# Issuing a weight load ahead of the last V part, an attention score ahead of a PV, and another order of masks, casts and zeroes on DVE and Pool

## Chip, cores, metric

One core of one Trainium2 chip. The metric is device time in microseconds (us) of one launch. Each execution also lists its mean granted TensorE clock (1.0 is full speed). All runs used here are of the state "fast" unless said otherwise; verdicts are given at 2%.

## The reference

Eight batches, eight heads, 576 positions, head size 64. Sliding-window causal attention (window 64), then an MLP on the 4608 rows of 512 with d_ff 2048:

```python
mask = (rel >= 0) & (rel < 64)
attn = softmax(where(mask, q @ k.T / 8, -1e9))
x = (attn @ v) as rows of 512           # 4608 x 512
h = x @ w_in                            # 512 -> 2048
out = (h * clip(h + 3, 0, 6) / 6) @ w_out
```

## The kernel before

The engines are TensorE (PE in the views; matmuls and transposes), VectorE (DVE), ScalarE (ACT) and GpSimd (Pool); the queue of SyncE (SP) issues transfers. A head's work is named by its step and its group g of two heads: T(g) transposes q and k, S(g) makes the scores, PV(g) multiplies them with V, *norm(g)* divides by the row sums, X(g) transposes the result. 576 positions are four parts of 128 and a rest of 64; the *V tail* is that last V part.

A planner in Python keeps a clock of each engine and decides from *estimated* durations on which engine a cast or copy goes, and in which order instructions are issued. The parts that matter:

```python
QK_ENG = ((('DVE', 'ACT'), ('ACT',), ('ACT',), ('ACT',)), (("DVE", "ACT"),) * 4)   # copies of the q/k transposes
SEQ = "ppppvvvppvpvpvvvvv" "wwwwwww" "PPPPww" "PPPPVVVVV"    # order of loads: p,v batch 0; w weights; P,V batch 1
ORDER = (... ('S1', 3), ('PV', 2), ('S0', 3), ('X', 0), ('PV', 3), ...)            # attention of batch 0
...
def tqk(b, g):                    # T(g): transposes of q and k, then one copy into QKT
    ...                           # 36 transposes, L582
    copy_op("spread", QK_ENG[b][g], 2 * S, pl.t + 0.1, QK_tiles[...], tr[...], ("tr", b, g))
...
def scores(b, g, which):          # S(g): waits for ("tr", b, g); exp on ACT; masks on DVE (L634, L638)
    pl.op("DVE", t, 1.3, fn, ("mask", b, g), deps=("mask",))
...
def scores64(b, gg):              # batches 2 to 7
    pl.op("DVE", t, 0.8, ..., ("mask", b, 2 * gg + a), deps=("mask64",))           # L683
    pl.op("ACT", pl.t + 0.1, 0.82, ex, ("exp", b, gg, part), msk if part else None)
...
def pv(b, g):                     # PV(g): waits for the mask and the V casts, then norm on DVE (L737, L740)
    pl.op("DVE", pl.t + 0.1, 1.05, norm, ("op", b, g), ..., deps=(("x", m // NG, m % NG),) if m >= 0 else ())
...
for T in range(NTB):              # nine MLP blocks of 512 rows
    s1(T)                         # first stage: 64 matmuls with W_in (L811), then relu and g
    s2(T, side)                   # second stage: 64 matmuls with W_out (L859), batch T+1's attention between them
```

The softmax here doesn't subtract the row's maximum and nothing guards it: scores larger than these inputs give would overflow.

## Time and profile before

| | before |
|---|---|
| median, three runs | 307.87 us (307.68 to 308.37) |
| profiled span, its mean clock | 307.3 us, 0.994 |
| TensorE busy | 96% |
| first MLP block starts (first L811) | 22.52 us |
| block 1 starts | 60.68 us |

Read it by the starts of the blocks: the *head* ends with the first L811, *block 0* with the second, and the *steady part* is the rest.

The stage table of before, one microsecond a row (length, then busy share and number of instructions of PE, PEld, DVE, ACT and Pool; the third number from the end is the granted clock, the last two are DMA share and GB/s), shows what it is:

```profile
8.00:9.00 1.00, 0.79 (x30) 0.79 (x32) 0.67 (x3) 0.00 (x0) 0.00 (x0) 0.56 1.06 347
9.00:10.00 1.00, 1.00 (x16) 0.37 (x11) 0.38 (x2) 0.58 (x1) 0.00 (x0) 0.50 1.13 333
```

The granted clock is 1.00 until 8 us and again from 12 us; with 0.56 and 0.73 in the rows at either end, TensorE had half its clock from about 8.1 to 11.5 us, for 3.4 us, in this one execution (of 309.16 us).

### The profile page before, as it was taken

The page shows a single profiled execution, that of the slowest core. Times are in us where ns is not written, and L with a number is a line of the kernel's source. Part 1 is how long each engine was busy: PE and PEld are TensorE (multiplying, and loading weights), DVE is VectorE, ACT ScalarE, POOL GpSimd, SP SyncE. Part 2 cuts the span into 40 slices and gives each one's busy share as a digit, 9 for nine tenths or more (in the row PEclk, how much of TensorE's full clock was granted, in tenths as well). Part 3 has the DMA queues.
Part 4 walks back from the last instruction along what each step waited for, and adds up shares of the span by engine and source line. Part 5 has one row for each costly group of instructions (what it writes and reads, how often), then busy time and mean ns, then how long its engine had stood idle before and what let it go on. Part 6 is the DMA issues. An engine that isn't in the chain of part 4 may idle for free.

```text
span 307.3 us, 6640 instructions
## 1 busy us (share of the span) xinstructions
PE 294.4 (96%) x2752; PEld 154.0 (50%) x2787; DVE 162.6 (53%) x209; ACT 155.1 (50%) x190; POOL 117.6 (38%) x185
## 2 busy tenths in 40 slices
PE   6989989999999999999999999999999999999995
PEld 2554445644544454875444544454665544444443
DVE  4585676757634663466437653766275617304600
ACT  5765488365606661566156714671367236316611
POOL 3166748628914660458127622674270000000000
PEclk9799999999999999999999999999999999999999
DMA  7999999999999989999699989999990730010011
GB/s 214 254 341 391 388 338 226 250 202 289 213 196 253 282 160 159 226 281 192 149 205 284 208 129 213 266 215 140 210 218 12 120 94 0 34 70 34 0 68 71
DMA packets 134863, 58.38 MB, mean 190 GB/s; under 512 B 117296, under 2 KB 124720, under 8 KB 134832
## 3 DMA queue, kind: packets, MB, share of 16 engines
q1 hardware_dynamic: 106560, 50.80, 72.7%
q10 hardware_dynamic: 28272, 7.15, 11.8%
q8 instruction: 22, 0.36, 0.5%
q14 instruction: 9, 0.07, 0.1%
HBM read 36.70 MB, written 9.44 MB: 150 GB/s over the span
## 4 chain that ended last, share of the span: by engine, by line
PE 72%; DMA 11%; SPq 5%; DVE 3%; POOL 3%; ACT 3%; issue 2%; ACTq 0%; POOLq 0%
PE ps L811 36%; PE acc L859 31%; DMA st<-in_moe_w_out_dram 5%; DMA st<-in_v_dram 3%; SPq L357 2%; PE ps L699 2%; ACT pT L678 2%; PE ps L672 2%; DMA xT<-opg 2%; SPq L332 2%; DVE opg L740 2%; SPq L415 1%; DVE pT L683 1%; POOL V L280 1%; POOL wout L280 1%
## 5 line engine op out<-in xcount | busy, mean ns | idle before, releaser
L823 DVE SCALAR_TENSOR_TENSOR gT<-t,ps 128x1024 bf16<-128x1024 bf16 x72 | 87.7, 1221 | 96.6 <-ACT t L820 96.6
L859 PE MATMUL acc<-wout,gT 128*128 128x512 bf16 (+2 forms) x560 | 127.8, 373 | 3.2 <-issue 2.1
L811 PE MATMUL ps<-xT,win 128*128 128x512 bf16 (+4 forms) x701 | 126.1, 340 | 0.4 <-DMA xT<-opg 0.2
L820 ACT ACTIVATE t<-ps,half 128x1024 bf16<-128x1024 f32 x72 | 80.0, 1114 | 48.7 <-PE ps L811 46.7
L811 PEld LDWEIGHTS <-win 128*128 128x128 bf16 x704 | 65.2, 98 | 59.8 <-issue 0.3
L859 PEld LDWEIGHTS <-gT 128*128 128x128 bf16 x592 | 54.6, 98 | 60.7 <-issue 0.3
L877 ACT COPY osb<-acc 128x512 f32<-128x512 f32 (+2 forms) x37 | 21.4, 579 | 76.1 <-PE acc L859 70.3
L280 POOL CAST runs<-st 64x512 bf16<-64x512 f32 (+1 forms) x49 | 30.7, 626 | 69.9 <-DMA st<-in_v_dram 59.9
L280 POOL CAST nat<-st 128x512 bf16<-128x512 f32 x48 | 32.5, 698 | 12.4 <-DMA st<-in_k_dram 8.3
L678 ACT ACTIVATE pT<-ps 128x768 bf16<-128x768 f32 x36 | 26.9, 834 | 9.3 <-PE ps L672 9.3
L683 DVE TENSOR_TENSOR pT<-pT,mask 128x1152 bf16<-128x1152 bf16 x24 | 21.6, 919 | 15.5 <-ACT pT L678 15.5
L740 DVE TENSOR_TENSOR opg<-ps,rec 128x640 bf16<-128x640 f32 x32 | 26.4, 825 | 1.1
L280 POOL CAST V<-st 128x512 bf16<-128x512 f32 (+1 forms) x30 | 19.2, 641 | 3.2 <-DMA st<-in_v_dram 1.6
L622 ACT ACTIVATE pT<-ps 128x768 bf16<-128x768 f32 x16 | 12.6, 825 | 1.0 <-PE ps L613 0.8
L699 PEld LDWEIGHTS <-pT 128*64 128x64 bf16 x480 | 8.9, 111 | 6.4 <-DVE opg L740 2.5
L279 ACT COPY QKT<-ps 128x1152 bf16<-128x1152 bf16 x8 | 9.0, 1124 | 6.1 <-PE ps L582 6.1
L699 PE MATMUL ps<-runs,pT 128*64 128x65 bf16 x288 | 10.8, 197 | 0.9 <-DVE pT L683 0.8
L277 DVE CAST runs<-st 128x576 bf16<-128x576 f32 x14 | 7.2, 519 | 7.9 <-DMA st<-in_q_dram 5.5
L699 PE MATMUL ps<-V,pT 128*64 128x65 bf16 x192 | 10.2, 198 | 0.0
L672 PEld LDWEIGHTS <-QKT 64*128 64x128 bf16 x432 | 7.3, 95 | 5.1 <-issue 4.7
L280 POOL CAST wout<-st 128x1024 bf16<-128x1024 f32 x6 | 7.4, 1253 | 5.9 <-DMA st<-in_moe_w_out_dram 5.9
L582 PE MATMUL ps<-ident,runs 64*64 64x64 bf16 x288 | 7.1, 199 | 2.6 <-DVE runs L277 2.5
(60 smaller groups left out, 123.2 us busy)
## 6 DMA issues: line engine op xcount, KB each, us to landing
out_dram<-osb SPq DMA_DIRECT2D x35, 256.0 KB, 3.8
st<-in_q_dram SPq DMA_DIRECT2D x12, 512.0 KB, 7.2
st<-in_k_dram SPq DMA_DIRECT2D x24, 256.0 KB, 6.6
st<-in_v_dram ACTq DMA_DIRECT2D x24, 256.0 KB, 5.4
st<-in_moe_w_out_dram SPq DMA_DIRECT2D x4, 1024.0 KB, 13.8
st<-in_moe_w_in_dram SPq DMA_DIRECT2D x3, 1024.0 KB, 11.6
st<-in_q_dram SPq DMA_DIRECT2D x8, 288.0 KB, 6.9
st<-in_k_dram SPq DMA_DIRECT2D x8, 288.0 KB, 6.9
```

The source lines that it names most:

```text
L280: return lambda s: nc.gpsimd.tensor_copy(out=out_ap, in_=in_ap) and None
L622: nc.scalar.activation(out=pT[:, :, kbs[0] : kbs[0] + 2, 0:QW], in_=st[:, :, 0 : 2 * QW].rearrange("p h (k w) -> p h k w", k=2), func=EXP, ...
L672: nc.tensor.matmul(st[:, h, c * D : (c + 1) * D], lhsT=kwin(b, g, i, h), rhs=turned(qk(b, 0, g), i)[h * D : (h + 1) * D], start=True, stop ...
L678: nc.scalar.activation(out=pT[:, :, part * NB * D : (part + 1) * NB * D], in_=st[:, :, 0 : NB * D], func=EXP, scale=scale,)
L683: pl.op("DVE", t, 0.8, lambda s: nc.vector.tensor_tensor(out=P_half, in0=P_half, in1=mask64[:].unsqueeze(1).unsqueeze(1).to_broadcast([P, ...
L699: nc.tensor.matmul(o[odd * D : (odd + 1) * D, h, m * VW : (m + 1) * VW], lhsT=pT[:, h, i * D : (i + 1) * D], rhs=(V if i % 2 else W)[:, g, ...
L740: nc.vector.tensor_tensor(out=opg[:].rearrange("p k h d -> p h k d"), in0=ov[:, :, :, 0:D], in1=rec[:].unsqueeze(3).to_broadcast([P, 2, KB ...
L811: nc.tensor.matmul(hs, lhsT=win16[:, g, (2 * c + j) * P : (2 * c + j + 1) * P], rhs=xs, start=(g == 0), stop=(g == NG - 1),)
L820: nc.scalar.activation(out=t1[:], in_=hT[:], func=RELU, bias=half[:], scale=1.0 / 6.0)
L823: nc.vector.scalar_tensor_tensor(out=gT[:, 2 * c : 2 * c + 2, :], in0=cell["t"][:], scalar=1.0, in1=hT[:], op0=MIN, op1=MULT,)
L859: nc.tensor.matmul(accs[ts][:, c0:c1], lhsT=gT[:, fc, ts * P : (ts + 1) * P], rhs=wout16[:, fc, c0:c1], start=(fc == 0), stop=(fc == NFC - 1),
L877: nc.scalar.copy(out=osb[:, c0:c1], in_=acc[:, c0:c1])
```

## The change

The intent: fill a hole in the transfers at 14 to 16 us with W_in's first part; give TensorE S(3)'s matmuls while the V tail arrives; keep Pool free for W_in casts; load batch 1's q and k ahead of the last W_out part; and put the last mask of a batch ahead of a normalisation that does not need it. The diff, with the unchanged part of ORDER and lines with only new times cut:

```diff
-SEQ = "ppppvvvppvpvpvvvvv" "wwwwwww" "PPPPww" "PPPPVVVVV"
+SEQ = "ppppvvvppvpvpvvvvwvwwwwww" "PPPPwPPwPP" "VVVVV"
-ORDER = (... ('S1', 3), ('PV', 2), ('S0', 3), ('X', 0), ...)
+ORDER = (... ('S1', 3), ('S0', 3), ('PV', 2), ('X', 0), ...)
-    at("POOL", 17.0, 0.3, lambda: nc.gpsimd.memset(mask32[:], 1.0))     # all of Pool's masks and zeroes: 17 -> 21
+    at("POOL", 21.0, 0.3, lambda: nc.gpsimd.memset(mask32[:], 1.0))
...
-        pl.op("POOL", 0.0, 0.3, ..., ("w1", i), deps=(("T", NR6 - 1, NG - 1),))
+        pl.op("POOL", 0.0, 0.3, ..., ("w1", i), deps=(("T", NR6 - 1, NG - 1), ("cast", NR6 - 1, 2, KB - 1)))
...
-                        ("DVE", "ACT", "POOL"), V[:ss, 2 * i : 2 * i + 2, kb, :, 0:D],
+                        ("DVE",) if (i, kb) == (1, KB - 1) else ("DVE", "ACT", "POOL"), V[:ss, ...],
...
-                            ("POOL",) if i else ("DVE", "ACT", "POOL"), win16[:, :, c0 : c0 + w2],
+                            ("POOL",) if i else ("POOL",), win16[:, :, c0 : c0 + w2],
...
-            pl.op("ACT", pl.t + 0.1, 0.82, ex, ("exp", b, gg, part), msk if part else None)
+            pl.op("ACT", pl.t + 0.1, 0.75, ex, ("exp", b, gg, part), msk if part else None)
...
+        first = (("mask", b, NG - 1),) if b >= NR6 and g == 1 else ()
         pl.op("DVE", pl.t + 0.1, 1.05, norm, ("op", b, g), None if b < NXP else xdma,
-              deps=(("x", m // NG, m % NG),) if m >= 0 else ())
+              deps=first + ((("x", m // NG, m % NG),) if m >= 0 else ()))
```

One line is added, so lines from L757 on are one higher in the changed kernel (L811 is L812, L859 is L860).

More of the change, by code (lines that the diff above doesn't have):

```diff
@@ L30 @@
 QK_ENG = ((('DVE', 'ACT'), ('ACT',), ('ACT',), ('ACT',)), (("DVE", "ACT"),) * 4)
-SEQ = "ppppvvvppvpvpvvvvv" "wwwwwww" "PPPPww" "PPPPVVVVV"
-ORDER = (('T', 0), ('T', 1), ('S0', 0), ('S1', 0), ('S1', 1), ('T', 2), ('S0', 1), ('PV', 0), ('S1', 2), ('T', 3), ('S0', 2), ('PV', 1), ('S1', 3), ('PV', 2), ('S0', 3), ('X', 0), ('PV', 3), ('X', 2), ('X', 1), ('X', 3))
+SEQ = "ppppvvvppvpvpvvvvwvwwwwww" "PPPPwPPwPP" "VVVVV"
+ORDER = (('T', 0), ('T', 1), ('S0', 0), ('S1', 0), ('S1', 1), ('T', 2), ('S0', 1), ('PV', 0), ('S1', 2), ('T', 3), ('S0', 2), ('PV', 1), ('S1', 3), ('S0', 3), ('PV', 2), ('X', 0), ('PV', 3), ('X', 2), ('X', 1), ('X', 3))
 X_ENG = ((('DVE',), ('DVE', 'ACT'), ('DVE',), ('DVE', 'ACT')), (("DVE", "ACT"),) * 4)
@@ L239 @@
         out=neg[:, 2 * QW : 2 * QW + D], in_=neg32[:, 0:D]) and None, "neg", deps=("neg32",))
-    at("POOL", 17.0, 0.3, lambda: nc.gpsimd.memset(mask32[:], 1.0))
-    at("POOL", 17.1, 0.8, lambda: band(mask32, 0.0), "mask32")
+    at("POOL", 21.0, 0.3, lambda: nc.gpsimd.memset(mask32[:], 1.0))
+    at("POOL", 21.1, 0.8, lambda: band(mask32, 0.0), "mask32")
     pl.op("DVE", 26.0, 0.2, lambda s: nc.vector.tensor_copy(out=mask[:], in_=mask32[:]) and None, "mask", deps=("mask32",))
-    at("POOL", 17.2, 0.2, lambda: nc.gpsimd.memset(m64[:], 1.0))
-    at("POOL", 17.3, 0.3, lambda: nc.gpsimd.affine_select(
+    at("POOL", 21.2, 0.2, lambda: nc.gpsimd.memset(m64[:], 1.0))
+    at("POOL", 21.3, 0.3, lambda: nc.gpsimd.affine_select(
         out=m64[:], in_=m64[:], pattern=[[1, D]], compare_op=ISGE, fill=0.0, base=D, channel_multiplier=-1))
-    at("POOL", 17.4, 0.3, lambda: nc.gpsimd.affine_select(
+    at("POOL", 21.4, 0.3, lambda: nc.gpsimd.affine_select(
         out=m64[:], in_=m64[:], pattern=[[-1, D]], compare_op=ISGE, fill=0.0, base=-1, channel_multiplier=1), "m64")
@@ L250 @@
     for i, t in enumerate(W_ring):
-        pl.op("POOL", 0.0, 0.3, lambda s, t=t: nc.gpsimd.memset(t[:, :, :, :, D:VW], 1.0) and None, ("w1", i), deps=(("T", NR6 - 1, NG - 1),))
+        pl.op("POOL", 0.0, 0.3, lambda s, t=t: nc.gpsimd.memset(t[:, :, :, :, D:VW], 1.0) and None, ("w1", i), deps=(("T", NR6 - 1, NG - 1), ("cast", NR6 - 1, 2, KB - 1)))
         pl.op("POOL", 0.0, 0.6, lambda s, t=t: nc.gpsimd.memset(t[0:D, :, 0, :, :], 0.0) and None, ("w0", i), deps=(("w1", i),))
@@ L256 @@
     for t in natural:
-        at("POOL", 17.0, 0.6, zero("POOL", t[S % P : P, :, KB - 1, :]))
+        at("POOL", 21.0, 0.6, zero("POOL", t[S % P : P, :, KB - 1, :]))
     dma = {"t": 2.2, "lag": 0.2, "v": 0.0}
@@ L420, in go @@
                     casts(("cast", b, 2, i, kb), land, [(
-                        ("DVE", "ACT", "POOL"), V[:ss, 2 * i : 2 * i + 2, kb, :, 0:D],
+                        ("DVE",) if (i, kb) == (1, KB - 1) else ("DVE", "ACT", "POOL"), V[:ss, 2 * i : 2 * i + 2, kb, :, 0:D],
                         st.rearrange("p (g h d) -> p g h d", g=2, h=2), 4 * D)])
```

## The prediction

> **What bounds the kernel now.** I read the page first, then the stage table, then the timelines of the stretches where the chain of waits leaves TensorE.
>
> ```profile
> PE 294.4 (96%) x2752; PEld 154.0 (50%) x2787; DVE 162.6 (53%) x209; ACT 155.1 (50%) x190; POOL 117.6 (38%) x185
> ...
> PE 72%; DMA 11%; SPq 5%; DVE 3%; POOL 3%; ACT 3%; issue 2%; ACTq 0%; POOLq 0%
> ```
>
> TensorE is busy for 294.4 of 307.3 us, so all idle time of it together is 12.9 us. The view of waits for TensorE says to whom it goes:
>
> ```profile
> PE ps L582 <- DVE runs L277: 2.5, 4, 1.2
> PE acc L859 <- issue: 2.1, 13, 0.2
> PE ps L895 <- DVE idle L204: 1.3, 1, 1.3
> PE ps L699 <- DVE pT L683: 0.8, 3, 0.3
> PE ps L764 <- DVE opg L740: 0.6, 1, 0.6
> PE ps L712 <- ACT pT L622: 0.5, 1, 0.5
> ```
>
> The 2% line is 6.2 us away. Of the rows above, the change touches L699 (0.8), L764 (0.6), L712 (0.5) and a part of L582; the 1.3 us at the start (L895) and the 2.1 of issue stay. So the room is about 3 to 4 us if everything went right.
>
> There are three stretches. **Head**, 0 to 22.5 us: attention of batch 0, ending when the first matmul of the first MLP block (L811) starts. **Block 0**, 22.5 to 60.7 us: the MLP of block 0, with batch 1's attention threaded into its second half; the chain of waits runs through DMA there (wout landing at 35.27, V of batch 1 landing at 51.73). **Steady part**, from 60.7 us: L811 takes 13.8 us a block, 64 matmuls of 0.216 us, and nothing of it can shrink.
>
> In the head the timeline of TensorE shows its last two waits:
>
> ```profile
> 20.33 0.23 PE L712 MATMUL ps<-V,pT 128*128 128x65 bf16 x2 [0.52 <-ACT pT L622]
> ...
> 22.23 0.45 PE L764 MATMUL ps<-ident,opg 128*128 128x128 bf16 x5 [0.62 <-DVE opg L740]
> ```
>
> PV(3) waits for its exp, and the last transpose X(3) waits for the normalisation of PV(3). The stage table, one microsecond a row (last two columns: DMA share, GB/s), shows a hole in the transfers just ahead of that:
>
> ```profile
> 13.00:14.00 1.00, 1.00 (x27) 0.48 (x20) 0.02 (x1) 1.00 (x3) 0.19 (x1) 1.00 0.97 198
> 14.00:15.00 1.00, 1.00 (x22) 0.63 (x23) 0.74 (x3) 1.00 (x2) 0.42 (x2) 1.00 0.53 113
> 15.00:16.00 1.00, 1.00 (x43) 0.85 (x44) 1.00 (x2) 1.00 (x2) 0.94 (x3) 1.00 0.85 235
> ```
>
> From 22 to 43 us the same column stands at 385 to 408 GB/s, so the hole costs transfers that are needed later. In the steady part, DVE's timeline in block 3 (a reciprocal and a multiply make one normalisation) and TensorE's answer to it:
>
> ```profile
> 145.94 0.21 DVE L737 RECIPROCAL rec<-ps 128x10 f32<-128x10 f32 x1
> 146.18 0.82 DVE L740 TENSOR_TENSOR opg<-ps,rec 128x640 bf16<-128x640 f32 x1
> 146.92 0.91 DVE L683 TENSOR_TENSOR pT<-pT,mask 128x1152 bf16<-128x1152 bf16 x1
> ...
> 147.89 0.22 PE L699 MATMUL ps<-runs,pT 128*64 128x65 bf16 x1 [0.28 <-DVE pT L683]
> ```
>
> The last mask stands behind the normalisation of PV(1), and PV(3) waits for it.
>
> **What the Trainium skill says.** "Perfetto Trace Analysis", section "Tensor Engine Instruction (MATMUL, LD_WEIGHTS)": ACT, DVE and GPSIMD are strict FIFO, so an instruction put ahead delays all behind it. The trace agrees: the mask above starts the moment the multiply ahead of it lets it. "SBUF — State Buffer", the entry "shared port pair" of its terms: DVE and GpSimd arbitrate for one pair of ports and the loser blocks for the whole instruction. It fits: a 128x512 V cast on Pool takes 0.61 us at 50.96 and 1.08 us at 51.78, beside a DVE mask with two SBUF inputs. "DMA: Bandwidth & Descriptors", section "Why small descriptors are slow (HBM only)": a fixed cost on each packet. The V loads come in 256 B rows, and 44 to 50 us, when they are the traffic, shows 74 to 267 GB/s against 388 before.
>
> **The change part by part.**
>
> *W_in's first part ahead of the V tail.* No bytes are added. In the queue's own timeline the tail issues at 12.63 us (1.12 us) and the first W_in part at 13.80. Exchanged, 512 KB of long rows enter the queue 1.2 us earlier, into the hole. The hole lacks (385-113) + (385-235) = 422 KB over 14 to 16 us, about 1.1 us at 385 GB/s; I expect most of it, 0.7 us, by which everything queued behind moves earlier. But TensorE in 22.5 to 36.5 us is matmul-bound, so this is worth something only to later loads.
>
> *The V tail then lands later, and is cast by DVE behind norm(1).* The instruction order shows norm(1) ahead of the tail cast. Norm(1) ended at 18.47, so the cast ends near 18.85, and PV(2) cannot start at 18.10 as now. S0(3) fills that place: its 0.49+0.34 us of matmuls move up to 18.03, and its exp from 19.46 to about 19.05, when ACT is free. PV(2) 18.85 to 19.45, norm(2) until 20.6, a copy 0.45, norm(3) 1.07 to about 22.1, against 22.17 now. DVE has lost the 0.69 us W_in cast, but the tail cast and the later PV(2) take most of that back. Head: gain 0.1 us.
>
> *Masks and zeroes of Pool later, W_in casts ahead.* Pool's constants are 3.6 us of work (16.18 to 19.8 us). After two casts of 1.04 they end near 22.5, ahead of the next W_in cast at 24.55. Neutral.
>
> *Block 0.* In the order of instructions T(2) of batch 1 comes after 22 rather than 26 matmuls of L859, its q and k are loaded ahead of the last W_out part, and the copy of its transposes moves from ACT to DVE, behind the first mask. The waits removed: 0.58 and 0.15 us ahead of T(2). The new ones: the last W_out part lands 1.5 us later (two 295 KB loads ahead of it), less the 0.7, and is needed after 24 matmuls; its Pool cast takes 1.04 to 1.56 us, so TensorE stands about 1 us there. And the copy on DVE has to sit out a mask pair (0.95+0.68 us) that begins when the q cast is done, near 45.7: it runs 47.2 to 48.6, where ACT now does it from 46.87 to 47.99. S(2) starts near 48.65 as now (48.60) with 28 matmuls of L859 behind it instead of 30, a debt of 0.43. V of batch 1, whose tail cast at 53.43 held PV(0), comes 0.7 earlier, and the memsets of 1.4 us no longer stand between its casts: that repays 0.4. Sum: about 0.
>
> *Last mask ahead of norm(1), batches 2 to 7.* PV(2) starts at 147.10 and PV(3) at 147.89; a PV takes 0.40 where nothing waits (0.80 for two in block 2). So 0.39 us are lost in block 3, in the same way 0.34 in block 1 (84.59 and 85.33), 0.17 in block 4, some 0.35 in block 5, 0 in blocks 2 and 6. In block 5 the next stage then waits 0.2 us for a transposing DMA, so that gain may be swallowed. I count 0.9 us. Norm(1) ends 0.8 us later, but its transfer stands behind a store (146.0 to 148.02 in block 3), so no transfer is later.
>
> Sum: 0.1 + 0 + 0.9 = 1.0 us, so **306.8 us**.
>
> **The rivals.**
> 1. *The hole in DMA is what mattered.* Filling it moves every later load 0.7 to 1.1 us, and block 0, gated by DMA (the chain names it for 11%), follows. For: the chain goes wout to V to PV(0). Against: the S(2) wait on DVE's copy. It would give 305.5 to 306.
> 2. *New waits take over in block 0.* If the W_in part doesn't land earlier, the last W_out part and the copy on DVE cost 1 to 1.3 us and eat the steady gain: 307.5 to 308.3. For: the strict order on DVE. Against: a hole that is plainly there.
> 3. *The V tail becomes the bound of the head.* 512 KB take 1.35 us at 385 GB/s; if the tail lands after 18.8 us instead of near 17, PV(2), PV(3) and the first MLP block move with it: 307.5 to 308.5.
>
> **Range and chances.** The steady 0.9 us is read off directly; block 0 can go from -0.8 to +1, the head from -0.5 to +0.3. That gives 305.5 to 308.1. Faster by over 2% needs 6.2 us, more than all the waits touched; slower by over 2% needs a stall that nothing here suggests. Chances: 0.02 faster, 0.97 within, 0.01 slower.
>
> **What would show it.** Right: no wait of L699 on DVE L683, PV(3) 0.40 after PV(2) in all blocks; over 250 GB/s in 14 to 15 us; the first L811 within 0.3 us of 22.5; S(2) of batch 1 waiting for DVE; the step to block 1's L811 within 0.5 us of 60.7. Wrong: that step a microsecond or more earlier (rival 1) or later (rivals 2 and 3), or waits for the transposing DMA at further blocks.

## More of the kernel before

One row of the page, the granted clock in 40 slices of the span, deserved more attention than I gave it when I predicted:

```profile
PEclk9799999999999999999999999999999999999999
```

The 7 in the second slice is in the head.

## The result

| | before | changed |
|---|---|---|
| median of four runs | 308.12 us (307.68 to 308.45) | 311.12 us (310.27 to 311.77) |
| ratio of fast runs | 1 | 1.0097, 95% interval 1.0067 to 1.0126 |
| profiled span, clock | 307.3 us, 0.994 | 309.5 us, 0.989 |

Ratios are the mean time of one kernel's fast runs over that of the other's fast runs of the same rounds, so not quite the ratio of the medians. The changed kernel is 3 us slower, within 2% but where 1 us faster was predicted.

The page of the changed kernel, and its view of waits for TensorE (total us, times, longest):

```profile
PE 298.5 (96%) x2787; PEld 153.7 (50%) x2787; DVE 163.9 (53%) x208; ACT 154.1 (50%) x189; POOL 119.4 (39%) x187
...
PEclk9999996999999999999999999999999999999999
...
PE 81%; DMA 12%; SPq 3%; DVE 2%; issue 1%; POOL 1%; ACT 0%; ACTq 0%
```

```profile
PE ps L582 <- DVE runs L277: 1.9, 3, 1.2
PE ps L613 <- DVE QKT L277: 1.9, 1, 1.9
...
PE ps L712 <- DVE V L277: 0.6, 1, 0.6
PE acc L860 <- POOL wout L280: 0.3, 1, 0.3
PE ps L812 <- DMA xT<-opg: 0.2, 1, 0.2
```

TensorE's idle time is 11.0 us against 12.9 before, although the kernel is slower: *busy* time has grown by 4.1 us for the same work. Part of this is records: the profile before has 2752 of the 2787 matmuls (both counts stand in the pages). The 2.1 us that its waits put to "issue" are most likely such gaps and no idling: of the 20 profiles here, the nine that lack 35 matmuls show 2.1 to 2.6 us of it, and the others none. Without them the idle time before is 10.8 us. The rest points to a lower clock. The wait of L699 for masks is gone, as predicted. A new wait of 1.87 us for a copy on DVE is there, and the dip in the clock row has moved to the seventh slice. TensorE's timeline at that place (start, duration, what, and in brackets the idle time before it and who ended it):

```profile
46.25 1.07 PE L582 MATMUL ps<-ident,runs 64*64 64x64 bf16 x36
49.19 0.88 PE L613 MATMUL ps<-QKT 64*128 64x192 bf16 x10 [1.87 <-DVE QKT L277]
50.00 1.46 PE L860 MATMUL acc<-wout,gT 128*128 128x512 bf16 x3
```

and DVE's:

```profile
44.84 1.15 DVE L277 CAST runs<-st 128x576 bf16<-128x576 f32 x1
45.91 1.41 DVE L634 TENSOR_TENSOR pT<-pT,mask 128x1536 bf16<-128x1536 bf16 x1
47.24 0.62 DVE L638 TENSOR_TENSOR pT<-pT,mask 128x128 bf16<-128x128 bf16 x1
47.79 1.34 DVE L277 COPY QKT<-ps 128x1152 bf16<-128x1152 bf16 x1
```

In the kernel before, ACT made that copy and S(2) did not wait:

```profile
46.87 1.12 ACT L279 COPY QKT<-ps 128x1152 bf16<-128x1152 bf16 x1 [1.60 <-PE ps L582]
48.60 0.53 PE L613 MATMUL ps<-QKT 64*128 64x192 bf16 x10
```

In the changed kernel the transposes of T(2) were done at 44.3 us, but their copy, which S(2) needs, stands on DVE behind a cast and a mask pair. T(3) is the last thing that TensorE has ahead of S(2); no MLP matmul is planned between the two, so from 47.3 us on it stands still. What comes after is worse than the wait itself. The stage table (columns as above):

```profile
47.00:48.00 1.00, 0.32 (x20) 0.20 (x13) 1.00 (x3) 0.61 (x1) 1.00 (x2) 1.00 1.08 226
48.00:49.00 1.00, 0.00 (x0) 0.00 (x0) 1.00 (x1) 0.51 (x1) 0.36 (x1) 0.71 1.02 219
49.00:50.00 1.00, 0.81 (x11) 0.59 (x11) 1.00 (x3) 0.27 (x1) 0.87 (x1) 0.50 0.77 165
50.00:51.00 1.00, 1.00 (x7) 0.43 (x4) 0.55 (x1) 1.00 (x2) 0.65 (x2) 0.50 1.11 317
```

The granted clock falls in the standstill, near 48.4 us, and stays at one half until about 55.3 us, 6.8 us in all; the next eight L860 matmuls take 0.44 us each instead of 0.216. The Trainium skill, "TensorE: Matmul & The Clock Gate", section "Part 1: The HAM clock gate", names half clock as the state after an idle window of about 3.4 us; here it came after 1.1 us of a standstill of 1.87 us, behind 1.07 us of transposes.

The hole in the transfers has moved and is not filled (stage table of the changed kernel):

```profile
14.00:15.00 1.00, 1.00 (x42) 0.82 (x38) 0.97 (x3) 0.70 (x1) 0.56 (x2) 1.00 0.73 189
15.00:16.00 1.00, 1.00 (x20) 0.51 (x16) 0.94 (x3) 1.00 (x3) 0.94 (x3) 1.00 1.07 365
16.00:17.00 1.00, 1.00 (x23) 0.58 (x19) 0.65 (x3) 1.00 (x2) 0.02 (x1) 1.00 0.87 197
```

And the V tail now gates PV(2), on DVE and TensorE:

```profile
17.74 0.97 DVE L277 CAST V<-tl 64x256 bf16<-64x256 f32 x1 [0.17 <-DMA tl<-in_v_dram]
```

```profile
18.77 0.19 PE L712 MATMUL ps<-V,pT 128*128 128x65 bf16 x1 [0.62 <-DVE V L277]
```

In the steady part the mask stands ahead of the normalisation, as intended (DVE in block 3):

```profile
149.49 0.75 DVE L683 TENSOR_TENSOR pT<-pT,mask 128x1152 bf16<-128x1152 bf16 x1
150.15 0.21 DVE L737 RECIPROCAL rec<-ps 128x10 f32<-128x10 f32 x1
```

From TensorE's timelines, the stages of both (worked out as differences between first instructions of stages):

| us | before | changed |
|---|---|---|
| first MLP block starts | 22.52 | 22.08 |
| block 0, second stage | 24.35 | 28.22 |
| block 1 starts | 60.68 | 64.14 |
| second stages of blocks 1 to 6 | 17.54, 17.18, 17.60, 17.34, 17.64, 17.17 | 17.13 each |

So block 0 lost 3.87 us, and the second stages of blocks 1 to 6 gave back 1.69 us, of which 1.27 us reached the end of the span.

### The profile page after: what moved, and what is told of

It reads as the page before. It is cut to its first block, busy times and chain, and to the rows that moved or that the text cites.

```text
span 309.5 us, 6682 instructions
## 1 busy us (share of the span) xinstructions
PE 298.5 (96%) x2787; PEld 153.7 (50%) x2787; DVE 163.9 (53%) x208; ACT 154.1 (50%) x189; POOL 119.4 (39%) x187
## 4 chain that ended last, share of the span: by engine, by line
PE 81%; DMA 12%; SPq 3%; DVE 2%; issue 1%; POOL 1%; ACT 0%; ACTq 0%
PE acc L860 38%; PE ps L812 36%; DMA st<-in_moe_w_out_dram 5%; PE ps L699 3%; PE ps L672 3%; DMA st<-in_q_dram 3%; DMA st<-in_k_dram 2%; DMA xT<-opg 1%; DMA tl<-in_v_dram 1%; SPq L415 1%; POOL wout L280 1%; SPq L332 1%; SPq L505 1%; PE ps L613 1%; DVE pT L634 0%
## 5 line engine op out<-in xcount | busy, mean ns | idle before, releaser
L860 PE MATMUL acc<-wout,gT 128*128 128x512 bf16 (+2 forms) x592 | 134.7, 378 | 0.4 <-POOL wout L280 0.3
L812 PE MATMUL ps<-xT,win 128*128 128x512 bf16 (+4 forms) x704 | 126.4, 340 | 0.2 <-DMA xT<-opg 0.2
L812 PEld LDWEIGHTS <-win 128*128 128x128 bf16 x704 | 65.1, 98 | 60.2 <-issue 0.6
L860 PEld LDWEIGHTS <-gT 128*128 128x128 bf16 x592 | 54.9, 98 | 62.7 <-issue 3.5
L683 DVE TENSOR_TENSOR pT<-pT,mask 128x1152 bf16<-128x1152 bf16 x24 | 20.8, 883 | 15.8 <-ACT pT L678 15.8
L699 PEld LDWEIGHTS <-pT 128*64 128x64 bf16 x480 | 8.6, 111 | 5.1 <-issue 3.4
L279 ACT COPY QKT<-ps 128x1152 bf16<-128x1152 bf16 x7 | 7.9, 1128 | 4.5 <-PE ps L582 4.5
L737 DVE RECIPROCAL rec<-ps 128x10 f32<-128x10 f32 x32 | 6.8, 213 | 6.1 <-PE ps L717 5.3
L699 PE MATMUL ps<-runs,pT 128*64 128x65 bf16 x288 | 9.9, 196 | 0.0
L280 POOL CAST win<-st 128x1024 bf16<-128x1024 f32 x8 | 8.1, 1039 | 4.0 <-DMA st<-in_moe_w_in_dram 4.0
```

The lines of the kernel that those rows point to most:

```text
L280: return lambda s: nc.gpsimd.tensor_copy(out=out_ap, in_=in_ap) and None
L683: pl.op("DVE", t, 0.8, lambda s: nc.vector.tensor_tensor(out=P_half, in0=P_half, in1=mask64[:].unsqueeze(1).unsqueeze(1).to_broadcast([P, ...
L699: nc.tensor.matmul(o[odd * D : (odd + 1) * D, h, m * VW : (m + 1) * VW], lhsT=pT[:, h, i * D : (i + 1) * D], rhs=(V if i % 2 else W)[:, g, ...
L812: nc.tensor.matmul(hs, lhsT=win16[:, g, (2 * c + j) * P : (2 * c + j + 1) * P], rhs=xs, start=(g == 0), stop=(g == NG - 1),)
L860: nc.tensor.matmul(accs[ts][:, c0:c1], lhsT=gT[:, fc, ts * P : (ts + 1) * P], rhs=wout16[:, fc, c0:c1], start=(fc == 0), stop=(fc == NFC - 1),
```

## The experiments

Eighteen runs, all correct. The kernel before ran beside them (medians 308.90, 308.89, 308.61, 308.73, 308.49 us). **Theory:** the copy on DVE behind the masks (A) and the clock drop after it are the loss. **Rivals:** W_out's later last part; the V tail in the head; or the mask gain being illusory.

*e1: the copies of T(2) and T(3) of batch 1 on ACT.*

```diff
-QK_ENG = (..., (("DVE", "ACT"),) * 4)
+QK_ENG = (..., (("DVE", "ACT"),) * 2 + (("ACT",),) * 2)
```

> The changed kernel with one thing undone: the copy of T(2)'s transposes of batch 1 is bound to ACT again, as in the kernel before. Theory A (the copy behind the mask on DVE makes TensorE stand still for 1.87 us before S(2), and the standstill is followed by about 7 us at half clock): both go, block 1's first L812 comes at about 60.3 us instead of 64.3, PEclk stays 1.0 between 40 and 60 us, time 306.0 to 307.0. Rival B (the loss is the later last part of W_out and the other load order): the start stays later than 61.5 us, time 308.5 to 310. Rival C (the clock dropped by chance in that one profile): 309 to 310.

Measured: 307.54 us median, ratio 0.9944 (0.9909 to 0.9979), two slow runs left out; the profile is of a slow run. No standstill, clock 1.00 throughout block 0. Its fast runs (mean 306.98) are 5.7 us shorter than those of the changed kernel (e4, mean 312.66). This speaks for A, but was too good: see e10. Block 1 starts at 62.29 us in the profile, later than the 60.3 that A expected (59.90 in e10); its second stage of block 0 is still 25.59 us.

*e2: eight idle matmuls in the gap between T(3) and S(2); the wait itself stays.*

```diff
+            if (b, g) == (1, 3):
+                fill = two_banks(["fill"])
+                for i in range(8):
+                    nc.tensor.matmul(fill[:, 0, :], lhsT=idle[:, 0:P], rhs=idle[:], start=True, stop=True)
```

> The changed kernel with 8 matmuls of 128x512 on a free PSUM slot put between T(3) of batch 1 and S(2), in the place where TensorE stood still; their result is used by nothing. The wait for DVE's copy stays. Theory A: the stall stays but the clock doesn't drop, so block 1 starts 2.5 to 3 us earlier than in the changed kernel, near 61.5 us, time 308 to 309. If the clock has nothing to do with the idle time (rival C), nothing is gained: time 311 or, with the 8 x 0.216 us added, up to 312.

Measured: 310.10 us, ratio 1.0043: below the 311 of rival C, but over the 308 to 309 that A expected. TensorE's timeline:

```profile
47.27 1.90 PE L907 MATMUL ps<-idle 128*128 128x512 bf16 x8
49.32 0.53 PE L613 MATMUL ps<-QKT 64*128 64x192 bf16 x10
49.78 1.47 PE L860 MATMUL acc<-wout,gT 128*128 128x512 bf16 x6
```

S(2) begins as late as before the filling (49.32), but takes 0.53 us instead of 0.88, the clock stays at 1.00, and block 0's second stage takes 25.57 us instead of 28.22. So in this profile useless work in the gap goes with no drop; executions of three such runs are counted below.

*e3: the kernel before, with only `first` added to the dependences of the normalisation.*

> The kernel before with one part of the change alone: norm(1) waits for the last mask in batches 2 to 7. If the steady part's gain of 1.26 us (246.46 to 245.2 us from block 1's first L811 to the end) is this order: 306.7 to 307.1, no wait of L699 on L683. If that gain came from transfers that moved: within 0.2 us of before.

Measured: 308.56 us, ratio 0.9994 (0.9947 to 1.0042), one slow run. The stages from block 1 on are 17.13 us each, as in the changed kernel; the time does not show it.

*e4: the changed kernel again.*

> The changed kernel unaltered, for a second profile. Theory A: TensorE stands still before S(2) for 1.5 us or more and PEclk is 0.5 for several us after it again, block 1 starts at 63.5 to 64.5. Rival C: the granted clock stays 1.0 there and block 1 starts near 61.5; the time of 311 then has another cause.

Measured: 313.25 us, ratio 1.0128. Standstill 1.88 us again; half clock for 3.4 us only; block 0's second stage 26.96 us.

**Single parts put into the kernel before, or taken out.**

*e5: the changed kernel with W_out's order put back, and the copies on ACT.* SEQ becomes `"ppppvvvppvpvpvvvvwvwwwwww" "PPPPww" "PPPPVVVVV"`.

> The changed kernel with two things undone in block 0: the last W_out part is loaded ahead of the q and k of T(2) again, and T(2)'s copy is bound to ACT again. Kept: the first W_in part ahead of the V tail, S0(3) ahead of PV(2), Pool's order, the last mask ahead of norm(1). Measure: the MLP of block 0 from its first L860 to block 1's first L812. If the W_out order is the second cost (theory A2: in e1 TensorE still waited 0.49 + 0.31 us for W_out's casts): it falls from 25.6 (e1) to 23.4 to 24.4, as in the two kernels with the old order (24.35, 23.38), time 1 to 2 us below the kernel before. If Pool's memsets or something else is the cost: it stays at 25 to 25.6 and the time at that of the kernel before.

Measured: 309.27 us, ratio 0.9994; block 0's second stage 25.34 us, no better than e1's 25.59, so W_out's order is not what costs there.

*e6: the kernel before with W_out's order alone.* SEQ becomes `"ppppvvvppvpvpvvvvv" "wwwwwww" "PPPPwPPwPP" "VVVVV"`.

> The kernel before with one part alone: q and k of T(2) are loaded ahead of the last W_out part (the copy stays on ACT, and T(2) moves 4 matmuls earlier). Theory A2: TensorE waits 0.5 to 1.5 us for W_out's casts and block 0's second stage takes 25 to 25.6 us against 23.4 to 24.35, time +0.5 to +1.5 us. Rival (the order is harmless): 23.4 to 24.4 and no change.

Measured: 309.06 us, ratio 0.9999 (0.9950 to 1.0049). TensorE waits 0.8 us for the last W_out casts, and no loss is seen (block 0's second stage takes 24.86 us, e3 and e11 23.38 and 24.65). The interval leaves room for 1.5 us; with e5, this rival has nothing for it.

*e7: the kernel before with the copy of T(2) of batch 1 on DVE.*

```diff
+QK_ENG = (..., (("DVE", "ACT"),) * 2 + (("DVE",), ("DVE", "ACT")))
```

> The kernel before with one part alone: T(2)'s copy of batch 1 is bound to DVE; the schedule puts it behind two masks there and 6 matmuls of L860 ahead of S(2). Theory A: TensorE stands still before S(2) for 0.5 to 2 us; if that is long enough PEclk falls to 0.5 behind it, and block 0's second stage is 1 to 4 us longer, time +1 to +4 us. Rival (the copy on DVE is harmless where the old load order is kept): within 0.5 us of the kernel before.

Measured: 310.14 us, ratio 1.0030 (0.9982 to 1.0078). S(2) waits 0.62 us and the clock does not drop: here six L859 matmuls happen to stand between T(3) and S(2). So the copy behind masks on DVE does its full harm only where TensorE has nothing else to do.

*e8: the kernel before with the mask order and S(3) ahead of PV(2).*

> The kernel before with the last mask ahead of norm(1) and S0(3) ahead of PV(2), nothing else. If these two are the good part of the change: the six stages with a batch at 17.13 us each, the first L812 at 22.0 to 22.5 us, block 0's second stage 23.4 to 24.4, time 1.5 to 2 us below the kernel before. If the order in the head is worth nothing: as e3.

Measured: 309.35 us, ratio 1.0036 (0.9981 to 1.0090). The planner also moved a W_in cast to ACT, so it is not a clean single part. It gave one thing: the first MLP block begins at 20.98 us, with the clock at 1.00 in the head. e6 gave 21.00, e11 20.97; e3 and e7, whose profiles have a drop at 8 to 12 us like before's, 22.49 and 22.55. So before's head is 21.0 us undisturbed, and a drop there costs 1.5 us.

*e9: the changed kernel, copy still on DVE but ahead of the mask pair.*

```diff
-                pl.op("DVE", t, 1.3, fn, ("mask", b, g), deps=("mask",))
+                pl.op("DVE", t, 1.3, fn, ("mask", b, g), deps=("mask",) + ((("tr", b, 2),) if b == 1 and g < 2 else ()))
```

> The changed kernel, with one thing altered: the first two masks of batch 1 wait for the copy of T(2)'s transposes, so that this copy, still on DVE, stands ahead of the mask pair and not behind it (the order of instructions on DVE shows that; nothing else on DVE changes until then, the planned order of TensorE shifts a little). Theory A (place: it is the mask pair of 1.41+0.62 us ahead of the copy that makes TensorE stand still for 1.87 us and drops its clock): no standstill over 0.8 us ahead of S(2) of batch 1, no L860 matmuls of 0.44 us there, block 0's second stage about 25.5 us as with the copy on ACT, time about that of the ACT version (within 1 us of it in this call). Rival (engine: DVE's copy is the cost as such, at 1.34 us against 1.12 us on ACT, and lies on TensorE's path wherever it stands): TensorE still waits over 1.3 us for it, the clock drops, and the time is 2.5 us or more above the ACT version.

Measured: 310.70 us, ratio 1.0054. As theory A says, the wait for the copy shrinks to 0.52 us and the clock stays at 1.00. But block 0's second stage takes 27.70 us all the same: the later masks and exps push an output copy on ACT, for which TensorE waits 1.07 us, and there are waits of 0.85 for g, 0.82 for W_out and 0.38 for V. The time is 1.3 us above e10's. Place and not engine makes the standstill; but in block 0 the waits replace each other.

*e10: e1 again.*

> The changed kernel with the copies of T(2) and T(3) of batch 1 on ACT, again, with five rounds, as the first time it was the only version that beat the kernel before (ratio 0.9944). Theory A and the gain of the mask order (1.7 us in the stages): ratio 0.993 to 0.998, interval below 1. Rival (the first result was luck of a spread of +-1.5 us between executions): ratio 0.999 or more. A point to see in its profile: with block 0 shorter, block 1 waits for the V casts of batch 2 on Pool (1.6 us the first time), which the changed kernel does not reach; if so again, that wait takes a part of what block 0 gives.

Measured: 309.41 us, ratio 1.0010 (0.9967 to 1.0053). e1's gain over before was luck of the draw. Block 0's second stage took 24.51 us here, 25.59 in e1: single profiles of one kernel differ by 1 us. The V wait in block 1 that I asked for did not come back (17.13 us). All twelve executions of e1 and e10 together, slow ones included, average 308.77 us; the 55 of before 308.76. So the copy on ACT takes back the whole loss, though the exchange is still in.

*e11: e3 again.*

> The kernel before with the mask order of batches 2 to 7 alone, again, with five rounds. The stage table of the first run shows 17.13 us in every second stage from block 1 on, 1.69 us less in sum than before. If the stages set the time: ratio 0.994 to 0.997. Rival (the gain is swallowed by waits for transposing transfers and V casts that it uncovers, as the first result of 0.9994 suggests): 0.998 to 1.001, with such waits of 1 us or more in sum in the first stages or block 1.

Measured: 308.01 us, ratio 0.9976 (0.9934 to 1.0017): between theory and rival, still not shown to be faster. Block 1 takes 15.20 and 18.00 us for its two stages instead of 13.81 and 17.13, so waits of 2.3 us are there, as the rival said.

*e12: the kernel before with W_in's first part ahead of the V tail, and nothing else.* SEQ becomes `"ppppvvvppvpvpvvvvwvwwwwww" "PPPPww" "PPPPVVVVV"`.

> The kernel before with only the first W_in part issued ahead of the last V part of batch 0; W_out, the engine choices, S(3) and the masks as before. Prediction's term: the hole in the transfers at 14 to 16 us is filled, head within 0.3 us, time 0 to 0.5 us less. Theory of the result (the hole only moves, rival 3 in part): a stretch under 250 GB/s somewhere in 14 to 18 us all the same, first L811 within 0.5 us of 22.5 apart from the clock of the head, ratio 0.998 to 1.003. If this part alone costs over 1 us (ratio above 1.004), a part of the loss of 3 us is the V tail's and not the copy's.

Measured: 312.63 us, ratio 1.0119 (1.0084 to 1.0155), a surprise. The first MLP block begins at 24.95 us. DVE's timeline:

```profile
21.57 0.69 DVE L277 CAST win<-st 128x1024 bf16<-128x1024 f32 x1 [3.12 <-DMA st<-in_moe_w_in_dram]
22.18 0.21 DVE L737 RECIPROCAL rec<-ps 128x10 f32<-128x10 f32 x1
```

The planner put a W_in cast ahead of the normalisation of PV(2), and DVE sat idle 3.12 us for its transfer with ready work behind it; TensorE waited 2.09 us for that normalisation and 1.27 us for the V tail's cast. So the exchange is harmful by itself where the planner places the casts. In the changed kernel, where W_in's casts are bound to Pool, the tail's cast to DVE and S(3) stands ahead of PV(2), these waits are 0 and 0.6 us; which of the three lines does it was not tried. And one more thing, which matters for the clock: from 17 to 23.4 us TensorE stood still for 1.27 and then for 2.09 us in this profile, the second time longer than ahead of S(2) in the changed kernel, and the clock stayed at 1.00:

```profile
22.00:23.00 1.00, 0.00 (x0) 0.00 (x0) 0.97 (x3) 0.00 (x0) 0.00 (x0) 1.00 1.04 399
```

**Fourth call.**

*e13: the changed kernel with the exchange undone alone.* SEQ starts `"ppppvvvppvpvpvvvvv" "wwwwwww"` again.

> The changed kernel with the exchange undone alone: the last V part of batch 0 is issued ahead of W_in's first part again; everything else of the change stays, the copy on DVE behind the mask pair too. If the exchange is what costs the head (theory): first L812 at 21.0 +-0.2 us where the clock does not drop, no wait of PV(2) on DVE's cast of the tail, time 0.7 to 1.2 us below the changed kernel run in this call; the standstill of 1.9 us ahead of S(2) stays. If the later head comes from the S(3) move or from the casts bound to engines (rival): first L812 at 21.5 to 22.5 us all the same, and the time is that of the changed kernel within 0.4 us.

Measured: 309.02 us, ratio 1.0001 (0.9960 to 1.0041), 1.0 us below e16 in the medians. The head ends at 21.53 us, PV(2) does not wait. What I did not expect: the standstill is gone too, with the copy still on DVE behind the same mask pair. DVE's and TensorE's timelines:

```profile
44.60 1.79 DVE L634 TENSOR_TENSOR pT<-pT,mask 128x1536 bf16<-128x1536 bf16 x1
...
46.92 1.34 DVE L277 COPY QKT<-ps 128x1152 bf16<-128x1152 bf16 x1
```

```profile
48.32 0.53 PE L613 MATMUL ps<-QKT 64*128 64x192 bf16 x10
```

The planner, with other load times, sends one more of the last q/k casts to Pool and none to DVE ahead of the mask pair; the mask pair begins 1.3 us earlier on DVE, T(3) comes later, and the two meet. The exchange at 13 us had thereby decided the order at 45 us.

*e14: e13 with the copies on ACT as well.*

> The changed kernel with both harmful parts undone: the exchange, and the copy of T(2) of batch 1 (on ACT now). What stays: W_out's order, S(3) ahead of PV(2), Pool's order, the masks. Sum of the theory's terms against the changed kernel: head -1.0, standstill -1.3 to -1.9, clock -0.5 to -0.7 (half of 1.3 to 1.5): 3 to 3.5 us below it, that is 307.5 to 308.5 against 308.7 before, ratio 0.994 to 0.999. Rival (the losses in block 0 replace each other, so that other waits take over): ratio 1.000 to 1.004, with waits of more than 2 us in sum in the second stage of block 0.

Measured: 308.70 us, ratio 1.0004 (0.9963 to 1.0044): both parts out, and it is level with before, in the rival's range, though the waits in block 0's second stage (25.06 us) sum to 1.3 us and not to over 2. Its six executions average 308.75 us, as those of e1, e5 and e10 do with the exchange in (308.78, 18 executions). So no cost of the exchange reaches the time here; with a spread of 1.5 us between executions, up to about 1 us can't be excluded.

*e15: the changed kernel with the mask order undone alone* (`first = ()` and the exp's estimate back to 0.82; e3 shows that `first` alone gives the new order; that the estimate does too, no run shows).

> The changed kernel with the mask order of batches 2 to 7 undone alone (no dependence of norm(1) on the last mask, and the scheduler's estimate of the exp back at 0.82 us; built, only the order of DVE's instructions in blocks 1, 3, 4 and 5 differs, with the buffers that PV(3) takes). If the stage table's 1.7 us reach the time: 1.2 to 1.8 us above the changed kernel run in this call, second stages of 17.2 to 17.7 us. If it is swallowed by waits for transposing transfers: within 0.5 us of it, and the first stages shorter in sum than those of the changed kernel by about as much as the second are longer.

Measured: 312.63 us against 310.03 for e16. But all four of its executions have a mean clock of 0.994 or less, and two of e16's four. With a drop: 312.62 against 311.74 on average, and against 312.25 for all six such executions of the changed kernel. Second stages of blocks 1 to 6: 104.6 us in sum against 103.0. So by this it is 0.4 to 0.9 us, between the two readings.

*e16: the changed kernel a third time.*

> The changed kernel a third time, as the yardstick of this call and for the clock. Expected: 310.5 to 313 us, ratio 1.006 to 1.013; standstill of 1.87 us ahead of S(2) in the profile; a drop of the granted clock behind it in about half of the executions (mean clock at or below 0.995), and executions with a drop 1 to 2 us longer than those without. If the drop were the main cause, executions without it would take 309 us or less.

Measured: 310.03 us, ratio 1.0057. Standstill 1.88 us, half clock behind it in the profile. Executions without a drop: 309.06 and 309.07; with one: 310.99 and 312.48.

**Is it idling, or want of plain matmuls, that lowers the clock?**

*e17: e2's filler as 32 transposes; e18: e2 again.*

```diff
-                fill = two_banks(["fill"])
-                for i in range(8):
-                    nc.tensor.matmul(fill[:, 0, :], lhsT=idle[:, 0:P], rhs=idle[:], start=True, stop=True)
+                fill = two_banks(["fill"], BF16)[:, 0, :]
+                for i in range(32):
+                    nc.tensor.transpose(out=fill[:, (i % 8) * P : (i % 8 + 1) * P], in_=idle[:, 0:P], identity=ident[:])
```

> The changed kernel with 32 idle 128x128 transposes in the gap between T(3) and S(2) of batch 1, in the place where the filler experiment had 8 plain matmuls; TensorE is busy through the gap either way, and the wait for the copy is the same. If the clock looks at busy time as such (theory: idle): no drop, clock 1.00 in the rows behind it, mean clock 0.998 or more in 5 of 6 executions, time as with the plain filler (about 310 us). If transposes do not count as work for it (rival, which the clock-gate page of the skill says of them): the drop comes as without any filler, mean clock 0.995 or less in about half of the executions and in the profile, time 1 us or more above the plain filler's.

> The changed kernel with 8 plain 128x512 matmuls on idle data in the gap, again, as the yardstick of this call: clock 1.00 in block 0's rows of the profile, mean clock 0.998 or more in 5 of 6 executions, 309.5 to 310.5 us, S(2) still waiting for the copy on DVE behind the filler.

Measured: e17 309.55 us (ratio 1.0032), e18 311.03 (1.0068). e17's timeline, where TensorE does nothing but transposes from 46.72 to 49.6 us:

```profile
47.71 1.96 PE L907 MATMUL ps<-ident,idle 128*128 128x128 bf16 x32
```

The clock stays at 1.00 there (this profile has a drop of 3.4 us elsewhere, from 20.5 us on, in the head, which had a wait of 1.36 us for the V tail), and five of six executions have a mean of 0.998 or more. So transposes held the clock as plain matmuls did: it is the standstill, and not the want of plain matmuls, that the drop followed. e18 came 0.5 us above what I expected; its profile has a wait of 1.36 us for a W_in cast and 18.89 us for block 1's second stage.

## Why the prediction was wrong

**How many executions drop, and what it costs.** A drop of some 3.4 us at half clock lowers the mean over 309 us by 0.0055, so executions split cleanly at 0.9975. The changed kernel: 6 of 12 with a drop, mean 312.25 us; 6 without, 310.50. The kernel before: 6 of 55, 309.36 against 308.68. The versions without the standstill: e2, e17 and e18 together 2 of 18, e1, e5, e10, e13 and e14 1 of 28. (The mean does not tell where a drop is; by the profiles, those of before, e3, e7 and e17 are in the head.) So the drop costs about 1.75 us where it happens (block 0's second stage with a drop of 3.4 us: 26.97, 28.00 and 27.01 in e4, e15 and e16, mean 27.33, against 25.57, 25.59 and 25.24, mean 25.47, with a filler in e2, e17 and e18), and makes about 0.8 us of the mean loss of 2.6 us (311.38 for all 12, against 308.76): without a drop the changed kernel is still 1.8 us slower. (Executions of several chips are pooled here; the medians of before differ by 0.4 us.) The first profile, with its longer drop (28.22), exaggerates it.

The experiments give the same division by time alone: the changed kernel 311.38 us, with a filler 310.27 (e2, e17, e18: 18 executions, 2 with a drop; the wait stays), with the copy on ACT 308.78 (e1, e5, e10: 18 executions, 1 with a drop, two slow ones included; no wait either; e5 has W_out's order back as well), before 308.76. So about 1.1 us of the loss go with the drop and 1.5 us with the wait, each with a standard error of half a microsecond.

**Point by point, by the prediction's steps:**

- *Head, "gain 0.1 us": failed in the stages; its worth in time is not shown.* Its baseline of 22.5 was an execution with a half clock at 8 to 11 us. Undisturbed heads: without the exchange 20.97, 20.98, 21.00, 21.12, 21.53 (mean 21.1); with the exchange in the form of the changed kernel (all such profiles but e17's, which has a drop in the head) 21.26 to 23.07 in ten, mean 22.0. So the head loses 0.9 us. The mechanism of rival 3 was there (0.6 us of wait for the tail's cast, and 1.0 us instead of 0.6 for normalisations), and the comparison hid it. The cast of the tail was predicted to end near 18.85 and ended at 18.71, but that is luck: norm(1) ended at 17.56 and not at 18.47, the cast then waited for its transfer, and took 0.97 us where I had put 0.38. But e14 against e1, e5 and e10 shows no time for it.
- *"Filling the hole": did not happen.* Predicted over 250 GB/s in 14 to 15 us; measured 189, and 197 two rows later. The third W_in cast, on Pool at 24.55 us in before, starts between 22.6 and 26.2 us in the other profiles, on average at 24.7 us with the exchange in the changed kernel's form and at 23.7 without it, so no gain to later loads is shown.
- *Block 0, "about 0": the step that failed.* S(2) was to start as now; TensorE stood still for 1.87 us ahead of it, for the copy on DVE. In the stages it is wrong by 1.3 us without a drop (25.47 against 24.13, the mean of 24.35, 23.38 and 24.65 in before, e3 and e11, whose change begins with batch 2), by 3.2 us with one. The debt of two matmuls (28 instead of 30 ahead of S(2)) is as counted in the traces. The term that was mis-sized is the copy: predicted 47.2 to 48.6, measured 47.79 to 49.13. The mask ahead of it began at 45.91 and not 45.7, and took 1.41 us, where I had put 0.95: a cast of Pool, 45.69 to 46.51, overlaps its start; it fits the exclusive port that I had named for V casts only: in the changed kernel, e4, e13 and e16 this mask ends 0.80 to 0.81 us after the end of the cast of Pool that it meets (here 47.32 after 46.51). From the start of the stage to S(2), 12.27 us became 13.27. The W_out wait, put at 1 us, is 0.3 (0.8 in e1 and e9). I had named the wait for the copy and did not ask what TensorE would do in it: with no matmul planned in the gap, the wait was a standstill, and in half of the executions it took the clock too.
- *Steady part, "gain 0.9 us": mechanism right, its size under- and its worth overestimated.* The second stages of blocks 1 to 6 gained 1.69 us, all 17.13 now. But the first stages wait for the transposing transfers. Over blocks 2 to 8, 15 profiles with the mask order have second stages (2 to 6) of 85.65 us in sum and first stages 1.46 us over 64 matmuls' time; five profiles without it have 86.62 and 0.55. The time from block 2 to the end is 211.6 against 211.7. The gain of 0.97 us in those blocks is swallowed, as I had feared for block 5 alone. In e4:

```profile
PE ps L812 <- DMA xT<-opg: 2.2, 4, 1.3
```

**The sum without a drop:** head +0.9, block 0 +1.3, steady about 0: +2.2 us. Measured: 310.50 − 308.68 = +1.8. **With a drop** of 3.4 us behind the standstill, +1.9 more (27.33 − 25.47): +4.1; measured 312.25 − 308.68 = +3.6. This is near, but no proof: by the same sum the copy on ACT should still lose 1.9 us (in e1, e5 and e10 the heads average 21.96 us and block 0's second stages 25.15), and those executions lose nothing. Sums of stages from single profiles are good to about 1 us; the executions decide, and they name the copy. Of the rivals, the second (new waits in block 0; 307.5 to 308.3) came true in kind, the third (the V tail; 307.5 to 308.5) in the stages; neither was large enough, and none had the clock in it. The range given was too narrow even by its own terms: 307.87 − 0.9 + 1 + 0.3 is 308.3 and not 308.1.

**What stays open.** Why one execution drops and the next does not: no profile caught this standstill without the drop. But e12 idled 2.09 us without one, so the length of a standstill alone does not decide. Nor does the drop begin at a fixed point of it: about 1.1 us into the standstill in the first profile, at S(2)'s first matmul in e4, and 0.2 and 1.0 us after it in e16 and e15. How large the mask order's net gain is: 0.1 us by the time from block 2 on, 0.4 to 0.9 by e15, all below the spread of the executions (the kernel before alone ranges from 307.1 to 311.5 us). No version tried is shown to beat the kernel before; e11 (0.9976) is nearest.

## What to carry to other kernels

Check the granted clock of a stage before using it as a baseline: one drop in a single profile was larger than the whole effect to be predicted. When a copy moves to a busier engine, ask what TensorE has to do until the copy is done; if nothing, add to the wait what the clock may cost after it. Where a planner places instructions from estimates, a load moved at 13 us can reorder the work at 45 us, and parts of a change cannot be priced one by one.

## What the Trainium skill lacked or had wrong

- "TensorE: Matmul & The Clock Gate", section "Part 1: The HAM clock gate": half clock is given for an idle window of about 3.4 us. Here standstills of 1.87 to 1.88 us, each after about 1 us of transposes, were followed by a granted clock of 0.50, for 3.4 us in three profiles and 6.8 us in one, in four profiles of four that have them; of all 16 executions of these two kernels 10 show a drop in their mean clock. A standstill of 2.09 us in e12 was followed by none. The page says that short idling between groups of matmuls can make the clock go back and forth (section "A second HAM failure mode: psum-queue depth-cycling"), but has no figure for such gaps. The 3.4 us of a drop agree with its window.
- The same page, section "Part 4: PE-mode transpose", says that full clock does not engage for transposes, which do not count as work in the same way. Here 36 and then 32 transposes in a row (46.72 to 49.6 us) kept the granted clock at 1.00; the same stretch with the 32 left out lost it. The trace does not tell which mode these transposes use.
